# Fetching two weight matrices with 40 DMAs of four row blocks each, instead of 96 DMAs of one block

## The chip, the cores and the metric

The kernel runs on one core of a Trainium2 chip. The metric is the device time of one execution in microseconds; the kernel before took 446.88 us (median of 3 runs, 446.81 to 447.64). The profile is of one execution, whose span from the first to the last instruction is 445.8 us.

## The reference

An mLSTM cell (batch 4, 8 heads, 768 steps, head dimension 40) is followed by a multiplicative feed-forward block on 3072 tokens of 320 features.

```python
for t in range(S):                      # the cell, per batch and head
    m_new = np.maximum(f_gate + m, i_gate)
    C = exp(f_gate + m - m_new) * C + exp(i_gate - m_new) * outer(v, k)
    n = exp(f_gate + m - m_new) * n + exp(i_gate - m_new) * k
    y[t] = sigmoid(o_gate) * (C @ q) / max(abs(n @ q), 1)

x = y.transpose(0, 2, 1, 3).reshape(3072, 320)
a, b = x @ w1, x @ w2                   # w1, w2: 320 x 1024
out = (a * b @ w3) @ w_out              # w3: 1024 x 1024, w_out: 1024 x 320
```

The four weight matrices arrive as 64-bit floats, everything else as 32-bit floats. The kernel therefore sees each weight as two 32-bit words, and turns them into 32-bit floats itself.

## The kernel before

The program works in steps of one block of 128 tokens. In each step TensorE does the cell of that block and some matmuls of the feed-forward part, while the loads for later steps run. Since `(a * b @ w3) @ w_out` equals `a * b @ (w3 @ w_out)`, the kernel computes `w3o = w3 @ w_out` once, in the steps in which the weights come in.

A piece of a weight matrix goes through four stations: a raw buffer in SBUF that a DMA fills (`raw_tile`), a scaling of its two words on ScalarE (`scale`), the joining into a 32-bit float on VectorE (`to_f32`), and for w3 a turn of its 32 x 32 squares on VectorE. There are four raw buffers.

```python
def raw_tile(n, pieces):
    raw = idle.pop(0) if idle else wst.tile([128, n, 2], U32, name="raw", tag="raw", bufs=4)
    for r, src in pieces:                       # one DMA for each piece, on the SyncE queue
        dst = raw[r].rearrange("p n two -> p (n two)")
        if len(src.shape) == 3:
            dst = dst.rearrange("p (m n) -> p m n", m=2)
        nc.sync.dma_start(out=dst, in_=src)
    return raw

def scale(raw, early):
    lo, hi = raw[:, :, 0], raw[:, :, 1].bitcast(FP)
    nc.scalar.activation(out=hi, in_=hi, func=AF.Prelu, scale=2.0 ** -111, alpha=2.0 ** 32)
    # ... lo on ScalarE too (on VectorE for the first three)
```

The squares of w3 are turned within 32 partitions, so the order of w3's columns and w_out's rows over the partitions is chosen to suit that: partitions 32j to 32j+31 hold rows of w_out from its j-th quarter, and columns of w3 from their j-th quarter. Each such group of 32 partitions ("square") is filled by a DMA of its own.

```python
CQ = DFF // 4                                   # 256
squares = [slice(32 * j, 32 * (j + 1)) for j in range(4)]

elif kind == "wo":                              # i = 0..7; 128 rows of w_out
    dst, pieces = wo[:, i, :], [(square, wo_d[j * CQ + i * 32:j * CQ + (i + 1) * 32, :])
                                for j, square in enumerate(squares)]
else:                                           # w3: i = 0..7, part = 0, 1; 64 rows of w3
    dst, pieces = None, [(square, w3_d[i * 128 + part * 64:i * 128 + (part + 1) * 64, cols(j * CQ, CQ)]
                          .rearrange("(m r) n -> r m n", m=2)) for j, square in enumerate(squares)]
pend.append((dst, raw_tile(dst.shape[-1] if dst is not None else CW, pieces), i, part))
```

The SyncE queue issues these DMAs in program order between the other loads of a step. The main loop, cut to the loads and to what touches the raw buffers:

```python
for s in range(len(n_up)):
    if B <= s + 3 < NU: load_u(s + 3)           # pw: two DMAs
    if s + 2 < NU:
        load(s + 2)                             # k, q, v (q only while s + 2 < 10)
        load_o(s + 2)
    # ... cell and feed-forward matmuls of the step; fold() runs w3 @ w_out for finished blocks
    if N_DVE <= s + 1 < NU: gated = turn(s + 1) # turns k and q on VectorE
    # ...
    for _ in range(n_cvt[s] if s < len(n_cvt) else 0):
        convert()                               # scale if that is not done, then to_f32 (and turn w3)
    if s >= ahead:                              # ahead = 9
        while pend and len(scaled) < 2: scale_next()
    if N_DVE <= s + 2 < NU: load_turned(s + 2)  # eight DMAs
    while todo and fetched < converted + (2 if s < 2 else 3 if s < ahead - 1 else 4):
        fetch(*todo.pop(0)); fetched += 1
```

Of the kernel before, what the change touches and what calls it, by code (L numbers as in the profile page):

```python
# [16 lines left out]
def kernel(  # L17
# [37 lines left out]
    DM = H * D  # L55
# [101 lines left out]
    wo = const.tile([128, FO, DM], FP, name="wo")  # L157
# [5 lines left out]
    w1_d, w2_d, w3_d, wo_d = (x.bitcast(U32) for x in (moe_w1, moe_w2, moe_w3, moe_w_out))  # L163
# [3 lines left out]
    def raw_tile(n, pieces):  # L167
        raw = idle.pop(0) if idle else wst.tile([128, n, 2], U32, name="raw", tag="raw", bufs=4)
        for r, src in pieces:
            dst = raw[r].rearrange("p n two -> p (n two)")  # L170
            if len(src.shape) == 3:
                dst = dst.rearrange("p (m n) -> p m n", m=2)
            nc.sync.dma_start(out=dst, in_=src)  # L173
        return raw

# [15 lines left out]
    def cols(c0, n):  # L191
        return slice(2 * c0, 2 * (c0 + n))
# [1 line left out]
    every = slice(0, 128)  # L194

    CQ = DFF // 4
    squares = [slice(32 * j, 32 * (j + 1)) for j in range(4)]
    pend, scaled = [], []

    def fetch(kind, i, part):  # L200

        if kind == "w12":
            c0 = part * CW
            if i < 2 * KF:
                wt, src = ((w1, w1_d), (w2, w2_d))[i // KF]
                ko = i % KF
                dst, pieces = wt[:, ko, c0:c0 + CW], [(every, src[ko * 128:(ko + 1) * 128, cols(c0, CW)])]
            else:
                dst, pieces = wr[:, c0:c0 + CW], [(slice(j * REM, (j + 1) * REM), src[KF * P:DM, cols(c0, CW)])
                                                  for j, src in enumerate((w1_d, w2_d))]  # L210
        elif kind == "wo":
            dst, pieces = wo[:, i, :], [(square, wo_d[j * CQ + i * 32:j * CQ + (i + 1) * 32, :])
                                        for j, square in enumerate(squares)]
        else:
            dst, pieces = None, [(square, w3_d[i * 128 + part * 64:i * 128 + (part + 1) * 64, cols(j * CQ, CQ)]
                                  .rearrange("(m r) n -> r m n", m=2)) for j, square in enumerate(squares)]
        pend.append((dst, raw_tile(dst.shape[-1] if dst is not None else CW, pieces), i, part))


# [241 lines left out]
    w3o_words = w3o.rearrange("p f d -> p (f d)").bitcast(U32).rearrange("p (n two) -> p n two", two=2)  # L461
    load(0, slice(0, 2))
    fetch("w12", 0, 0)
    load(0, slice(2, 3))
    fetch("w12", 1, 0)
    load_o(0)
    fetch("w12", 2, 0)
    idle += [w3o_words[:, i * CW:(i + 1) * CW] for i in range(2)]
    fetch("w12", 3, 0)
# [360 lines left out]
```

## Time and profile before

| what | value |
|---|---|
| time | 446.88 us (446.81 to 447.64) |
| span of the profiled execution | 445.8 us |
| mean granted TensorE clock | 0.981 |
| moved by DMA | 52.72 MB, mean 118 GB/s |
| SyncE queue's packets under 512 bytes, of all 136555 | 109936 |
| VectorE busy, ScalarE busy | 306.3 us, 149.3 us |

The page gives busy times by engine, then rows of 40 equal slices of the span (11.1 us each), in which a digit is a busy share in tenths; then the DMA queues, the chain of work that ended last, the costliest groups of instructions, and the DMA issues with the KB of one and the median time from issue to landing. Queue q1 is SyncE's, q10 ScalarE's. PE is TensorE, DVE VectorE, ACT ScalarE, POOL GpSimd and SPq the queue of SyncE, where the issuing of a DMA is what takes time. L173 is the line of the `dma_start` in `raw_tile`, L180 the first scaling on ScalarE.

### The profile page before, as it was taken

The numbers are of one execution on the slowest core, as the hardware profiler recorded it, in microseconds if no ns is written. First come the engines' busy times: TensorE is split into PE (matmuls) and PEld (weight loads), VectorE is DVE, ScalarE is ACT, GpSimd is POOL, SyncE is SP. The second block draws the span as 40 slices with busy tenths as digits, with TensorE's granted clock in tenths as the row PEclk, the third lists the DMA queues.
The fourth block names the chain that finished last, engine by engine and source line by source line (L and its number), as shares of the span: only waits on it lengthen the run. The fifth ranks groups of instructions, "written<-read, shape, count | busy, mean of one in ns | idle before, by whom it ended". The sixth has DMA issues, their size and how long they took to land.

```text
span 445.8 us, 12871 instructions
## 1 busy us (share of the span) xinstructions
PE 423.7 (95%) x5271; PEld 335.5 (75%) x5271; DVE 306.3 (69%) x639; ACT 149.3 (34%) x407; POOL 81.7 (18%) x154
## 2 busy tenths in 40 slices
PE   4768989898999999999999999999999999999997
PEld 3656877787878878787877877778778777777774
DVE  5578387668866976696677949668699776444800
ACT  3766465445752454253212321213211111101110
POOL 3344043233211220222022203202020000000000
PEclk9995899999999999999999999999999999999999
DMA  8999989778988798697366466364111120000001
GB/s 203 182 175 201 200 142 170 172 176 166 205 198 186 147 180 177 161 165 140 83 116 148 102 132 140 76 136 109 50 35 35 39 46 16 15 16 15 1 30 44
DMA packets 136555, 52.72 MB, mean 118 GB/s; under 512 B 109936, under 2 KB 127536, under 8 KB 136496
## 3 DMA queue, kind: packets, MB, share of 16 engines
q1 hardware_dynamic: 132896, 47.87, 53.7%
q10 hardware_dynamic: 3600, 4.03, 2.7%
q8 instruction: 41, 0.67, 0.7%
q14 instruction: 18, 0.15, 0.1%
HBM read 46.07 MB, written 5.80 MB: 116 GB/s over the span
## 4 chain that ended last, share of the span: by engine, by line
PE 80%; DMA 5%; SPq 5%; ACT 3%; DVE 2%; POOL 2%; issue 2%; DVEq 0%; POOLq 0%
PE cell L92 22%; PE pa L92 18%; PE po L92 14%; PE pb L92 12%; PE wp L92 8%; PE p L92 5%; SPq L173 2%; SPq L128 2%; DMA raw<-in_moe_w_dram 2%; DMA o_in<-in_o_gate_dram 1%; DMA kbuf<-in_k_dram 1%; PE px L95 1%; POOL pw L279 1%; ACT pw L277 1%; ACT raw L180 1%
## 5 line engine op out<-in xcount | busy, mean ns | idle before, releaser
L92 PE MATMUL pa<-xT,w 128*128 128x256 f32 x240 | 62.1, 391 | 0.6 <-ACT xT L437 0.6
L92 PE MATMUL po<-w3o,ab 128*128 128x320 f32 x224 | 61.8, 433 | 0.0
L92 PEld LDWEIGHTS po<-w3o,ab 128*128 128x128 f32 x224 | 42.4, 190 | 17.3 <-issue 0.4
L306 POOL TENSOR_TENSOR state<-state,decay 128x164 f32<-128x164 f32 x40 | 19.7, 492 | 182.5 <-DVE den L387 168.2
L92 PEld LDWEIGHTS pa<-xT,w 128*128 128x128 f32 x240 | 45.7, 195 | 8.5 <-ACT xT L437 1.0
L92 PE MATMUL pb<-xT,w 128*128 128x256 f32 x192 | 45.9, 382 | 2.3 <-ACT kT L296 2.3
L583 DVE TENSOR_TENSOR ab<-pb,a_sb 128x512 f32<-128x512 f32 x24 | 16.6, 692 | 43.6 <-ACT a_sb L582 43.6
L279 POOL TENSOR_SCALAR_AFFINE_SELECT pw<-pw 64x512 f32<-64x512 f32 x48 | 34.4, 717 | 52.9 <-ACT pw L277 48.3
L92 PE MATMUL cell<-w3o,ab 128*128 128x320 f32 x160 | 44.0, 432 | 0.0
L92 PEld LDWEIGHTS pb<-xT,w 128*128 128x128 f32 x192 | 36.7, 192 | 8.2 <-ACT kT L296 3.1
L277 ACT ACTIVATE pw<-pw,aT 128x64 f32<-128x64 f32 x160 | 40.2, 336 | 2.8 <-ACT o_sb L685 2.8
L582 ACT ACTIVATE a_sb<-pa 128x512 f32<-128x512 f32 x24 | 14.3, 598 | 76.3 <-PE pb L92 76.3
L92 PEld LDWEIGHTS cell<-w3o,ab 128*128 128x128 f32 x160 | 30.4, 190 | 12.0
L630 DVE SCALAR_TENSOR_TENSOR a_sb<-pa,wo 128x512 f32<-128x512 f32 x12 | 8.3, 692 | 43.2 <-PE pa L92 43.2
L92 PE MATMUL pa<-xT,wr 64*64 64x256 f32 x384 | 36.8, 386 | 0.0
L92 PE MATMUL pb<-xT,wr 64*64 64x256 f32 x384 | 36.2, 379 | 0.0
L92 PE MATMUL wp<-wo,w3T 128*128 128x320 f32 x128 | 35.8, 432 | 0.0
L379 DVE TENSOR_TENSOR h<-cell,h 64x164 f32<-64x164 f32 x96 | 31.3, 326 | 1.8
L92 PEld LDWEIGHTS wp<-wo,w3T 128*128 128x128 f32 x128 | 23.7, 190 | 8.9
L92 PEld LDWEIGHTS pa<-xT,wr 64*64 64x64 f32 x384 | 19.0, 132 | 14.4 <-issue 8.4
L685 ACT COPY o_sb<-po 128x320 f32<-128x320 f32 x14 | 6.0, 427 | 67.4 <-PE po L92 67.4
L92 PEld LDWEIGHTS pb<-xT,wr 64*64 64x64 f32 x384 | 20.2, 133 | 3.0
(128 smaller groups left out, 722.8 us busy)
## 6 DMA issues: line engine op xcount, KB each, us to landing
raw<-in_moe_w_dram SPq DMA_DIRECT2D x64, 128.0 KB, 3.4
pw<-U_d SPq DMA_DIRECT2D x40, 128.0 KB, 3.7
kbuf<-in_k_dram SPq DMA_DIRECT2D x24, 160.0 KB, 4.5
vbuf<-in_v_dram SPq DMA_DIRECT2D x24, 160.0 KB, 5.1
o_in<-in_o_gate_dram SPq DMA_DIRECT2D x24, 160.0 KB, 4.8
out_dram<-o_sb ACTq DMA_DIRECT2D x24, 160.0 KB, 1.8
raw<-in_moe_w_dram SPq DMA_DIRECT2D x7, 512.0 KB, 5.6
raw<-in_moe_w_out_dram SPq DMA_DIRECT2D x32, 80.0 KB, 2.3
```

The lines of the kernel that those rows point to most:

```text
L92: in_order(nc.tensor.matmul(out, lhsT=lhsT, rhs=rhs, start=start, stop=stop))
L95: in_order(nc.tensor.transpose(out, in_, ident[0:n, 0:n]))
L128: nc.sync.dma_start(out=dst, in_=rows(src, n))
L173: nc.sync.dma_start(out=dst, in_=src)
L277: nc.scalar.activation(out=pw[:, h, :], in_=src[:, h, :], func=AF.Exp, bias=aT[:, c, b * H + h:b * H + h + 1])
L279: nc.gpsimd.affine_select(out=pw[r], in_=pw[r], compare_op=OP.is_ge, fill=0.0, base=0, pattern=[[0, H], [1, L]], channel_multiplier=-1)
L306: nc.gpsimd.tensor_tensor(out=new, in0=old, op=OP.mult, in1=decay[:, b * NP:(b + 1) * NP, 2 * c + x:2 * c + x + 1] .to_broadcast([P, NP, D1]))
L379: nc.vector.tensor_tensor(out=part, in0=ph[x][halves[e]], in1=part, op=OP.add)
L582: nc.scalar.mul(out=a_sb, in_=pa, mul=UP ** -2)
L583: nc.vector.tensor_tensor(out=ab_t[gr][j][:, fs[0]:fs[-1] + 1, t0:t0 + a_sb.shape[-1]], in0=pb, in1=a_sb, op=OP.mult)
L630: nc.vector.scalar_tensor_tensor(out=out, in0=p, scalar=UP ** -2, in1=q, op0=OP.mult, op1=OP.add)
L685: nc.scalar.copy(out=o_sb, in_=po)
```

## The change

The four DMAs of a w_out piece become one, and the four of a w3 piece become two. The source of each has three steps: the block j of four, the row of 32 within it, and the words of the row. The target is simply the 128 partitions with one run of words in each; the three-step source walks through it in the same order. For w3 the two halves m of a raw buffer (rows 0 to 31 and 32 to 63 of the piece) are each a DMA. It is meant to save the SyncE queue the issuing of 56 DMAs. The bytes, the runs of contiguous words and their places in SBUF are the same as before, and so is every instruction on the compute engines.

```diff
         for r, src in pieces:
-            dst = raw[r].rearrange("p n two -> p (n two)")
-            if len(src.shape) == 3:
-                dst = dst.rearrange("p (m n) -> p m n", m=2)
+            dst = (raw[:, r] if len(src.shape) == 3 else raw[r]).rearrange("p n two -> p (n two)")
             nc.sync.dma_start(out=dst, in_=src)
 ...
-    squares = [slice(32 * j, 32 * (j + 1)) for j in range(4)]
 ...
         elif kind == "wo":
-            dst, pieces = wo[:, i, :], [(square, wo_d[j * CQ + i * 32:j * CQ + (i + 1) * 32, :])
-                                        for j, square in enumerate(squares)]
+            dst, pieces = wo[:, i, :], [(slice(0, DM), wo_d.rearrange("(j c) n -> j c n", j=4)[:, i * 32:(i + 1) * 32, :])]
         else:
-            dst, pieces = None, [(square, w3_d[i * 128 + part * 64:i * 128 + (part + 1) * 64, cols(j * CQ, CQ)]
-                                  .rearrange("(m r) n -> r m n", m=2)) for j, square in enumerate(squares)]
+            dst, pieces = None, [(slice(m * CQ, (m + 1) * CQ), w3_d[r0:r0 + 32, :].rearrange("r (j n) -> j r n", j=4))
+                                 for m, r0 in enumerate(range(i * 128 + part * 64, i * 128 + (part + 1) * 64, 32))]
```

As built, the source of a w_out DMA is 4 x 32 x 640 words (steps 163840, 640, 1) and its target 128 x 1 x 640; the source of a w3 DMA is 4 x 32 x 512 words (steps 512, 2048, 1) and its target 128 x 1 x 512. Before, both sides were 32 x 640 for w_out and 32 x 2 x 512 for w3. The order of the instructions on the other queues does not change.

## The prediction

> **What bounds the kernel now.** I read the page first, for which engine fills the span and what the DMA queues carry. The trace then gave three further views: busy time by stretch, the timeline of the SyncE queue (which issues nearly every load), and the timeline of ScalarE, where the arriving weight pieces are first touched.
>
> ```profile
> span 445.8 us, 12871 instructions
> PE 423.7 (95%) x5271; PEld 335.5 (75%) x5271; DVE 306.3 (69%) x639; ACT 149.3 (34%) x407; POOL 81.7 (18%) x154
> ...
> DMA  8999989778988798697366466364111120000001
> ...
> q1 hardware_dynamic: 132896, 47.87, 53.7%
> q10 hardware_dynamic: 3600, 4.03, 2.7%
> ...
> PE 80%; DMA 5%; SPq 5%; ACT 3%; DVE 2%; POOL 2%; issue 2%; DVEq 0%; POOLq 0%
> ...
> raw<-in_moe_w_dram SPq DMA_DIRECT2D x64, 128.0 KB, 3.4
> ...
> out_dram<-o_sb ACTq DMA_DIRECT2D x24, 160.0 KB, 1.8
> ...
> raw<-in_moe_w_out_dram SPq DMA_DIRECT2D x32, 80.0 KB, 2.3
> ...
> gates<-in_i_gate_dram ACTq DMA_DIRECT2D x3, 32.0 KB, 2.0
> ```
>
> TensorE is busy for 95% of the span and makes 80% of the chain. The DMA row says that this isn't the whole story: for the first half of the span the 16 DMA engines are busy for seven to nine tenths of each slice, and in the last third hardly at all. So the kernel is bound by TensorE, with a first half in which the DMA engines are not far behind. The pieces that the change touches (64 issues for w3, 32 for w_out) all lie in that half.
>
> ```profile
> core 0: us, PE busy (x) PEld busy (x) DVE busy (x) ACT busy (x) POOL busy (x), PEclk, DMA share, GB/s
> ...
> 31.50:40.00 8.50, 7.27 (x167) 6.28 (x159) 6.40 (x17) 5.14 (x14) 1.83 (x3) 0.50 1.04 181
> ...
> 57.80:68.20 10.40, 9.06 (x177) 7.86 (x178) 8.94 (x19) 6.19 (x17) 4.65 (x8) 1.00 0.78 150
> ...
> 89.00:101.00 12.00, 12.00 (x206) 10.34 (x204) 7.97 (x19) 5.93 (x17) 3.66 (x6) 1.00 0.79 178
> ...
> 143.40:158.80 15.40, 15.40 (x225) 12.48 (x219) 11.58 (x24) 6.50 (x17) 3.31 (x6) 1.00 0.77 169
> ```
>
> The columns end with the granted clock, the DMA share and GB/s. From 112.5 us a step of the loop takes 15.4 us and TensorE fills all of it, with the DMA engines at about 0.8: the margin is a fifth.
>
> ```profile
> 57.82 5.53 SPq L173 DMA_DIRECT2D raw<-in_moe_w_out_dram x8
> ...
> 106.64 8.54 SPq L173 DMA_DIRECT2D raw<-in_moe_w_dram x16
> ...
> 183.73 3.60 SPq L173 DMA_DIRECT2D raw<-in_moe_w_dram x8
> ```
>
> ```profile
> 120.30 0.68 ACT L180 ACTIVATE raw<-raw 128x512 f32<-128x512 f32 x1 [1.46 <-DMA raw<-in_moe_w_dram]
> ...
> 194.18 0.67 ACT L184 ACTIVATE raw<-raw 128x512 uint32<-128x512 uint32 x1
> 194.75 0.45 ACT L437 COPY xT<-px 128x384 f32<-128x384 f32 x1
> ```
>
> The first w_out pieces are called for at 57.82 us, the last w3 pieces at 183.73. ScalarE scales each piece in program order, so a piece that comes late stops everything behind it on ScalarE, such as the copies that empty TensorE's banks. At 120.30 us it already waited 1.46 us for a w3 piece. There is little room for later landings.
>
> **What the Trainium skill says.** The page "DMA: Bandwidth & Descriptors", section "Why a DMA increments its semaphore by 16 and not by 1", has the decisive statement: a DMA is split over the largest number k of engines, at most 16, that divides the size of the slowest dimension (not of size 1) of both access patterns, and with a smaller k it uses the lowest-numbered engines. The trace of before fits k = 16 for every DMA. The ScalarE queue has 24 stores of 128 rows and 3 loads of 32 rows, 3168 rows; the page counts 3600 packets, and the 432 left are 27 issues times 16, one completion packet for each engine. The slowest dimensions there are 128 and 32. No DMA of the kernel before has a slowest dimension below 16, so nothing in it shows a smaller k. The section "Rules for kernel authors" of that page pulls both ways: it says to join many small transfers, which is what the change does, and to keep an outermost dimension that is a multiple of 16. The page "TensorE: Matmul & The Clock Gate", Part 1, says that the TensorE clock falls to half after an idle window of about 3.4 us; the stretch from 31.5 us above has 0.50, so long waits for data cost twice here.
>
> **The change part by part.**
>
> *Issues.* w_out goes from 32 issues to 8, w3 from 64 to 32: 56 fewer. The w3 issues take 3.60 us for eight in the timeline, 0.45 us each, so 25 us of the SyncE queue's time are saved. The chain has SPq at 5%, 22 us, of which the weight pieces' line L173 is 2%, 9 us. At most those 9 us could leave the path; more likely 3 to 5, as other waits end close by.
>
> *Engines per DMA.* The new source of a w_out piece is 4 x 32 x 640 words, that of half a w3 piece 4 x 32 x 512, with j = 4 outermost; the target has 128 partitions outermost. The largest number that divides 4 and 128 is 4. By that rule every new DMA runs on engines 0 to 3 alone. Bytes and rows stay: 1024 rows of 2560 bytes for w_out, 4096 of 2048 bytes for w3.
>
> *What a row costs one engine.* The trace has a record of each packet. The fastest tenth of the 2048-byte ones took 84 ns or less, of the 2560-byte ones 100 ns; the median of the 640-byte ones is 32 ns and the mean of the 160-byte ones 19 ns. A w_out piece has 128 rows: on 16 engines 8 rows each, 0.8 us; on 4 engines 32 rows, 3.2 us. A w3 piece (512 KB) has 256 rows: 16 rows each, 1.3 us, against 64 rows, 5.4 us.
>
> *What else these four engines carry.* Until the turned loads begin, a step loads k, q, v and o (4 x 1024 rows over 16 engines, 4 x 64 x 19 ns = 4.9 us) and the weights pw (2 x 64 rows, 8 x 84 ns = 0.7 us): 5.6. Later it is k, v, o (3.65), the turned k and q (1024 rows of 640 bytes, 64 x 32 ns = 2.05) and pw: 6.4 us. A later step with two w3 pieces therefore needs 10.8 + 6.4 = 17.2 us of engines 0 to 3, against 2.7 + 6.4 = 9.1 before and against TensorE's 15.4. Four engines become the bound while twelve stand idle.
>
> *The sum.* I treat engines 0 to 3 as one queue that is free at about 60.5 us (the o load issued at 56.87 has landed about then). Behind it come 8 w_out pieces, 26 us; 16 w3 pieces, 86 us; three early steps of other loads, 17 us; six later ones, 38 us. That makes 167 us, so the last w3 piece is through at about 228 us, and landed some 2 us after that. Before, its issue ended at 187.3 us and it landed in 3.4: 190.7. So it comes 39 us later. What can be absorbed: ScalarE's scaling starts 1.8 us after the landing, and the copy of px that follows (194.75) is needed by TensorE only when its banks come round, which I read as 4 to 5 us later. 39 less about 6 is 33 us. Freed issue time takes nothing off in a stretch that waits for four engines, and after the last piece the kernel is bound by TensorE as before. 446.9 + 33 = 480 us. Stalls at half clock may add a little: 481.
>
> It should not come evenly. The three single or double w_out steps add 2 to 4 us each; the worst is the sixteen-issue stretch at 106.64, where four w3 pieces come together: 21.6 us of engines 0 to 3 instead of 5.4. From there every step should be near 17 us instead of 15.4.
>
> **The rivals.**
> - *All 16 engines are kept.* Speaks for it: nothing in the trace shows a smaller k, and the transfer could be cut along the 128 target partitions. Then 25 us of SyncE time go, landings move little, and the time is 441 to 447 us. I give this about one in eight.
> - *Four engines, but hidden.* The loads run two steps ahead, four buffers hold w3, and once TensorE binds, DMA has a fifth to spare. If slack of 20 us is built up by 190 us, the loss is only 15 to 20: about 465. Against it: the 1.46 us wait at 120.30 and DMA shares near 0.8.
> - *Worse than the queue.* SyncE issues in order[...]; the early loads in the timeline took up to 4.81 us to issue one DMA (vbuf at 12.23). Loads of k, v and o would then wait behind w3 also where they are needed first, buffers come free late, and bubbles add to the 167 us. With TensorE at half clock: 495 to 515.
>
> **Range and chances.** Four engines give 465 to 510 by these; the working says 481. Sixteen engines give a result near 444. I leave that as the tail below the range: 457 to 510. Faster by over 2% needs 9 us, all that L173 has in the chain: 0.03. Within 2%: 0.12. Slower: 0.85.
>
> **What would show it.** Packets of the SyncE queue: 420 issues of 16 completion packets each lie in the 132896. With 4 of them for each of 40 new issues and 16 for the other 324 it is 131520; with 16 for all, 132000. The landing of a 256 KB w3 DMA: above 6 us for four engines, near 4 for sixteen. The DMA share between 60 and 220 us: lower than now although DMA binds, as twelve engines idle. The chain: DMA of raw and ScalarE's L180 in it, TensorE well below 80%. Steps near 17 us from 130 us on. I'm wrong if the packets come to 132000, or if they come to 131520 and the steps stay at 15.4 us.

## The result, and the profile after

The changed kernel took 496.52 us (median of 6 runs, 495.51 to 498.64) against 447.31 us before (446.81 to 448.03): a ratio of 1.110, with a 95% interval of 1.108 to 1.113. It is 49 us slower. The prediction said 481, in a range of 457 to 510.

The page of the changed kernel, cut to the rows that answer to those shown of before:

```profile
span 494.9 us, 12784 instructions
...
PE 433.6 (88%) x5271; PEld 340.3 (69%) x5271; DVE 305.2 (62%) x639; ACT 150.7 (30%) x407; POOL 81.7 (16%) x154
...
DMA  8999855545244544545567667365321111000001
...
q1 hardware_dynamic: 131520, 47.86, 43.9%
q10 hardware_dynamic: 3600, 4.03, 2.4%
...
PE 59%; DMA 15%; SPq 9%; DVE 5%; POOL 5%; issue 3%; ACT 3%; DVEq 0%; ACTq 0%; POOLq 0%
```

The SyncE queue has 131520 packets, to the packet the number for four completion packets on each of the 40 joined DMAs; 132000 would have meant sixteen. From the sixth slice to the 19th the DMA row has fallen to 4 or 5 tenths (once 2), where it had mostly 7 to 9, although the kernel now waits for DMA: the joined transfers leave most of the engines unused. TensorE's part of the chain fell from 80% to 59%, and DMA and SyncE rose to 24% together.

The busy time by stretch, three consecutive steps and the one before them (last columns: granted clock, DMA share, GB/s):

```profile
core 0: us, PE busy (x) PEld busy (x) DVE busy (x) ACT busy (x) POOL busy (x), PEclk, DMA share, GB/s
...
129.00:158.00 29.00, 17.38 (x219) 13.62 (x212) 11.60 (x23) 8.89 (x22) 3.31 (x6) 0.82 0.43 119
158.00:175.00 17.00, 15.64 (x215) 12.27 (x211) 11.59 (x23) 6.44 (x18) 3.31 (x6) 1.00 0.53 135
175.00:195.70 20.70, 17.23 (x219) 13.52 (x215) 11.59 (x23) 6.69 (x18) 3.31 (x6) 0.92 0.46 121
195.70:216.00 20.30, 17.43 (x219) 13.70 (x215) 11.60 (x23) 6.69 (x18) 3.31 (x6) 0.92 0.48 129
```

A step of 15.4 us has become one of 17 to 21, and the step that waits for four w3 pieces (129 to 158 us) takes 29. In the slow steps the clock is below 1, which is why TensorE is busy for 17 us with the same matmuls.

ScalarE's timeline shows what the steps wait for. The bracket is the idle time before an instruction and what ended it:

```profile
201.80 0.68 ACT L178 ACTIVATE raw<-raw 128x512 f32<-128x512 f32 x1 [2.57 <-DMA raw<-in_moe_w_dram]
...
207.64 0.68 ACT L178 ACTIVATE raw<-raw 128x512 f32<-128x512 f32 x1 [4.57 <-DMA raw<-in_moe_w_dram]
...
221.16 0.71 ACT L178 ACTIVATE raw<-raw 128x512 f32<-128x512 f32 x1 [1.69 <-DMA raw<-in_moe_w_dram]
...
226.64 0.67 ACT L178 ACTIVATE raw<-raw 128x512 f32<-128x512 f32 x1 [4.24 <-DMA raw<-in_moe_w_dram]
```

ScalarE now waits for both w3 pieces of these steps (L178 is the former L180). It takes up the two pieces of a pair 5.84 and 5.48 us apart, close to the 5.4 us of 64 rows on one engine. Such waits at this line add up to 47.8 us, where the kernel before had 2.4.

The timeline of the SyncE queue over one such step, from one call for w3 to the next:

```profile
153.93 2.60 SPq L171 DMA_DIRECT2D raw<-in_moe_w_dram  x4
156.64 1.81 SPq L148 DMA_DIRECT2D pw<-U_d  x2
158.50 0.58 SPq L128 DMA_DIRECT2D kbuf<-in_k_dram  x1
159.18 6.05 SPq L128 DMA_DIRECT2D vbuf<-in_v_dram  x1
165.27 3.53 SPq L142 DMA_DIRECT2D o_in<-in_o_gate_dram  x1
168.85 2.00 SPq L137 DMA_DIRECT2D gates<-in_k_dram  x4
170.90 1.85 SPq L137 DMA_DIRECT2D gates<-in_q_dram  x4
172.86 2.60 SPq L171 DMA_DIRECT2D raw<-in_moe_w_dram  x4
```

The queue has no gap of more than 0.11 us in these 18.9 us, though it issues four DMAs fewer than before. One issue for v takes 6.05 us and one for o 3.53. The same two in a step with w3 of the kernel before:

```profile
159.28 0.54 SPq L128 DMA_DIRECT2D vbuf<-in_v_dram  x1
159.86 1.49 SPq L142 DMA_DIRECT2D o_in<-in_o_gate_dram  x1
```

There v takes 0.53 or 0.54 us in all steps with two w3 pieces, and o 1.09 to 2.71. Against the shortest such issues, 0.53 and 0.37 us, some 8.7 us of the step are blocked. The semaphore records of the trace show what the blocked issues wait behind: in the five steps from here on, v's issue ends 0.2 to 0.5 us before the step's third w3 DMA has landed (165.23 and 165.45 us in this one), and o's 0.4 to 0.5 us after the fourth has (168.80 and 168.33). I read this as the lists in which the work of the four engines waits (their rings) being full; the trace does not name them.

### The profile page after: what moved, and what is told of

It is laid out like the page before. It is cut to its first block, busy times and chain, and to the rows that moved or that the text cites. A ratio compares the mean times of both kernels' runs of the same rounds, so it can differ in the third digit from the quotient of the medians.

```text
span 494.9 us, 12784 instructions
## 1 busy us (share of the span) xinstructions
PE 433.6 (88%) x5271; PEld 340.3 (69%) x5271; DVE 305.2 (62%) x639; ACT 150.7 (30%) x407; POOL 81.7 (16%) x154
## 3 DMA queue, kind: packets, MB, share of 16 engines
q1 hardware_dynamic: 131520, 47.86, 43.9%
## 4 chain that ended last, share of the span: by engine, by line
PE 59%; DMA 15%; SPq 9%; DVE 5%; POOL 5%; issue 3%; ACT 3%; DVEq 0%; ACTq 0%; POOLq 0%
PE cell L92 18%; PE pa L92 13%; PE po L92 12%; DMA raw<-in_moe_w_dram 10%; PE pb L92 8%; PE p L92 4%; POOL pw L275 3%; SPq L142 2%; DMA raw<-in_moe_w_out_dram 2%; SPq L137 2%; SPq L171 2%; PE wp L92 2%; SPq L128 2%; DMA o_in<-in_o_gate_dram 1%; DVE h L375 1%
## 5 line engine op out<-in xcount | busy, mean ns | idle before, releaser
L92 PE MATMUL pa<-xT,w 128*128 128x256 f32 x240 | 69.0, 424 | 25.7 <-ACT xT L433 24.1
L92 PEld LDWEIGHTS pa<-xT,w 128*128 128x128 f32 x240 | 49.7, 214 | 37.8 <-ACT xT L433 26.9
L92 PE MATMUL pb<-xT,w 128*128 128x256 f32 x192 | 49.0, 401 | 16.4 <-ACT kT L292 16.4
L92 PEld LDWEIGHTS pb<-xT,w 128*128 128x128 f32 x192 | 38.7, 203 | 23.5 <-ACT kT L292 17.6
L92 PEld LDWEIGHTS po<-w3o,ab 128*128 128x128 f32 x224 | 42.4, 190 | 17.3 <-issue 0.4
L178 ACT ACTIVATE raw<-raw 128x512 f32<-128x512 f32 (+1 forms) x32 | 20.2, 631 | 64.6 <-DMA raw<-in_moe_w_dram 47.8
```

What stands on the lines that cost most here:

```text
L92: in_order(nc.tensor.matmul(out, lhsT=lhsT, rhs=rhs, start=start, stop=stop))
```

## The experiments

Twelve runs of eleven kernels were made, in four batches, each batch beside runs of the kernel before on its own chip. Where totals differ by a few us only, I also compare the time between two marks of ScalarE's timeline, the copy of step 5 and the first one of step 16: the start-up before the first mark varies by some 4 us between runs, and the weights come in between the two. Before, that is 60.92 to 219.72, 158.8 us; after, 58.74 to 268.87, 210.1 us.

**Is it the number of engines? 40 DMAs of other shapes.** The joined DMAs keep their number, size, rows and three-step sources, but the outermost step counts 16, 8 or 4.

```diff
-wo_d.rearrange("(j c) n -> j c n", j=4)[:, i * 32:(i + 1) * 32, :]
+wo_d[i * 128:(i + 1) * 128, :].rearrange("(c j) n -> j c n", j=16)      # 8, 4
-w3_d[r0:r0 + 32, :].rearrange("r (j n) -> j r n", j=4)
+w3_d[i * 128:(i + 1) * 128, cols((2 * part + m) * CQ, CQ)].rearrange("(c j) n -> j c n", j=16)   # 8, 4
```

The weights then stand in another order in SBUF; nothing is left out.

> The changed kernel with the same 40 DMAs of the same sizes and rows, each with a source in three steps, but 16 x 8 rows instead of 4 x 32 (weights arrive in another order, so the output is not the reference's). If the DMA engines taken are the largest number that divides both outermost sizes, 16 are used: 443 to 448 us, 132000 packets on the SyncE queue. If a source in three steps, or joining pieces as such, is what costs, nothing improves: 490 to 500 us.

> The same with 8 x 16 rows. By the count of engines: 8 are used, 131680 packets on the SyncE queue; a w3 piece costs each of them 2.7 us, a later step 5.4 + 6.4 = 11.8 us, under TensorE's 15.4, so most is hidden: 447 to 456 us. If three steps as such cost: 490 to 500 us.

> Control for the kernels with 16 x 8 and 8 x 16 rows: the same choice of rows as theirs, but 4 x 32. If only the count of engines matters, it is like the changed kernel, 493 to 500 us, 131520 packets. If those were faster for their choice of rows: 450 to 465 us.

Measured: 452.6 us with 16 (ratio to before 1.009, interval 1.006 to 1.012), 464.1 with 8 (1.039, 1.033 to 1.045), 507.6 with 4 (1.130, 1.125 to 1.135). The page's line of the SyncE queue, for 16, 8 and 4 in this order:

```profile
q1 hardware_dynamic: 132000, 47.86, 54.2%
```

```profile
q1 hardware_dynamic: 131680, 47.86, 51.1%
```

```profile
q1 hardware_dynamic: 131520, 47.86, 43.9%
```

All three counts are those of the rule. The packet records of the traces show the engines at work too. Rows of 2560 bytes are w_out's alone. Between 60 and 250 us, whenever any of them is moving, four or five are moving at once for 29.0 of 35.0 us in the changed kernel, and hardly ever more than six; with 8 outermost it is eight or nine for 13.5 of 24.5 us; with 16 it goes up to 19. (The records of one engine overlap a little.) In the changed kernel's burst, from 126 to 139 us, several w3 DMAs wait together, and four or five rows move for 12.9 of the 13.0 us: the DMAs of this queue share the same four engines.

Three steps in a source cost nothing like 49 us; the engines do. Sixteen engines come out 5 us above what I expected. Eight engines lose 17 us, also more: in the profiled run, the slowest of four, the steps 9 to 11, which wait for the four w3 pieces called for together and for what queues behind them, take 17.0, 21.6 and 21.2 us, and from step 12 on they take 15.4. So the steady steps are hidden as worked out (11.8 us of work in 15.4), but the burst is not. The control with 4 is 11 us above the changed kernel, and above the range expected; it differs from it in the rows that an engine reads. That difference stays open.

**Is it joining, after all? Small DMAs on four engines.** The kernel before, with its 96 DMAs and nothing joined, but sources of 4 x 8 rows.

```diff
-wo_d[j * CQ + i * 32:j * CQ + (i + 1) * 32, :]
+wo_d[j * CQ + i * 32:j * CQ + (i + 1) * 32, :].rearrange("(c f) n -> f c n", f=4)
-w3_d[i * 128 + part * 64:i * 128 + (part + 1) * 64, cols(j * CQ, CQ)].rearrange("(m r) n -> r m n", m=2)
+w3_d[i * 128 + j * 32:i * 128 + (j + 1) * 32, cols(part * CW, CW)].rearrange("(c f) n -> f c n", f=4)
```

> The kernel before with its 96 small DMAs, nothing joined, but each with a source in three steps, 4 x 8 rows, so that 4 divides both outermost sizes and no larger number does (weights arrive in another order; w3's rows are 4096 bytes here, half as many). If the engines taken by a DMA are the whole cause, it is about as slow as the changed kernel: 485 to 500 us, with 129696 packets on the SyncE queue. If joining the pieces were the cause: 446 to 449 us.

Measured: 496.9 us (1.111, 1.105 to 1.117), as slow as the changed kernel, with

```profile
q1 hardware_dynamic: 129696, 47.86, 44.9%
```

as expected for four completion packets each. With the run of 16 outermost this settles the cause from both sides: joined on sixteen engines is within 1% of before, unjoined on four is all of the loss.

**Which matrix?** One part of the change at a time.

> Only w_out's pieces are joined, w3 as before. By the count of engines: 8 pieces of 3.2 instead of 0.8 us, 19 us more on engines 0 to 3 in the steps between 57 and 110 us, half of it hidden: 452 to 460 us, 132416 packets. If the whole loss comes from w3: 446 to 449 us.

> Only w3's pieces are joined, w_out as before. By the count of engines: 16 pieces of 5.4 instead of 1.3 us, 65 us more on engines 0 to 3, of which what TensorE's steps hide goes off: 478 to 490 us, 132000 packets. The two parts alone should add up to about the whole 49 us; if they share one wait they add up to more.

Measured: w_out alone 459.8 us (1.028, 1.026 to 1.031), 12.5 us above its own before of 447.3; w3 alone 489.7 us (1.095, 1.090 to 1.100), 42.4 above, both within the ranges expected and with the packets expected. Together 55 us, a little more than the 49 of both, which fits waits that the two share.

**Is TensorE's clock part of it?** TensorE is busy for 433.6 us instead of 423.7 with the same instructions. Extra matmuls, which nothing reads, were put where it stood still.

```diff
+if warm and (p is pb) == warm[0][1]:
+    for _ in range(warm.pop(0)[0]):
+        mm(cell[1][:, 0, 400:512], ident, ident[:, 0:112])
```

> The changed kernel with 352 extra matmuls of 112 columns, into a part of a bank that nothing reads, where TensorE stood still in steps 7, 9, 10, 12, 13 and 15. The changed kernel's TensorE is busy 9.9 us longer than before with the same instructions. If that is the half clock after each stall and lies on the path, the time falls by 6 to 10 us, to 486 to 491, with TensorE's granted clock back near 0.98. If the loads cover it: 496 to 499 us.

The first run was a miss: 524.9 us (1.172, 1.170 to 1.174). Its extra matmuls took 0.226 us each and outlasted the stalls; in step 7 the 58 took 13.1 us, for a stall of 6. It tells nothing about the clock. The second had 134 of them, sized by that duration.

> The run with extra matmuls again, with 134 of them instead of 352: one took 0.226 us and not the 0.095 us that it was sized by, so that the extra work outlasted the stalls it should fill. Now it is a little shorter than each stall of the changed kernel. If the half clock after a stall lies on the path: 486 to 491 us with a granted clock near 0.98. If not: 496 to 499 us.

Measured: 500.2 us (1.115, 1.111 to 1.119), no gain, though between 59 and 253 us the granted clock is 0.96, where the changed kernel has 0.90. Two of TensorE's waits in it:

```profile
153.26 1.99 PE L92 MATMUL pa<-xT,w 128*128 128x256 f32 x8 [1.32 <-ACT xT L433]
172.77 3.58 PE L92 MATMUL pa<-xT,w 128*128 128x256 f32 x8 [3.82 <-ACT xT L433]
```

Step 10 (153.26) starts at full clock after a wait of 1.32 us, where the changed kernel had waited 11.62 us and then ran its eight matmuls in 3.71. From the mark in step 5 to that of step 10 it took 95.4 us instead of 99.0. But the next step waits 3.82 us for the loads, in which the changed kernel waited 0.78, and from mark to mark both take 210 us. What the clock gives, the loads take back. My reading that the slow clock costs time of its own fell.

**Does the order of issues matter?** In the changed kernel, w3 is called for before the eight turned loads of the same step, instead of after them.

```diff
+        while todo and fetched < ...: fetch(*todo.pop(0)); fetched += 1
         if N_DVE <= s + 2 < NU:
             load_turned(s + 2)
-        while todo and fetched < ...: fetch(*todo.pop(0)); fetched += 1
```

> The changed kernel with a step's w3 pieces called for before its eight turned loads. SyncE takes 3.85 us to issue the turned loads, which keep an engine busy for 2.05, so engines 0 to 3 may run dry before w3 is called for. If they do, steps come down by up to 1.8 us and the time to 486 to 491 us. If engines 0 to 3 never run dry: 495 to 498 us.

Measured: 489.7 us (1.093, 1.089 to 1.097), 7 us below the changed kernel. From mark to mark it takes 200.0 us, 10 less. But the last ten w3 pieces still come at 18.8 us a pair, against 19.2 in the changed kernel (by ScalarE's starts on them), so most of the gain comes once, up to the burst of four pieces, and not as 1.8 us in each step: the time falls into the range expected, but not in the way expected. The timeline and the waits of its SyncE queue show why:

```profile
168.51 2.91 SPq L171 DMA_DIRECT2D raw<-in_moe_w_dram  x4
171.46 4.50 SPq L137 DMA_DIRECT2D gates<-in_k_dram  x4
176.00 7.56 SPq L137 DMA_DIRECT2D gates<-in_q_dram  x4
183.67 1.14 SPq L148 DMA_DIRECT2D pw<-U_d  x2
```

```profile
SPq L137 <- DMA raw<-in_moe_w_dram: 36.0, 18, 3.2
```

Now the turned loads are the blocked ones, 12.06 us for eight issues that take 3.85 in the changed kernel, and here the trace names the w3 transfers as what ended 36 us of those waits (between 100 and 240 us). They are waits for a semaphore: in the trace SyncE's DMAs use eight semaphores in turn, and an issue waits until the DMA of eight issues before has landed. Those at 176.91, 180.46 and 183.25 us start 0.02 us after a w3 DMA's last increment. So this is another wait than that of v and o above. VectorE waits for the turned loads in turn (3.6 to 6.5 us a step), and frees the raw buffers later. The blocking moves; it does not go.

**Another queue.** The joined DMAs are called for by GpSimd, so that their issues are no longer in SyncE's order.

```diff
-nc.sync.dma_start(out=dst, in_=src)
+(nc.gpsimd if len(src.shape) == 3 else nc.sync).dma_start(out=dst, in_=src)
```

> The changed kernel with its 40 joined DMAs called for by GpSimd instead of SyncE; all else the same. In the changed kernel SyncE stands for about 8.6 us of each 18.9 us step at issues that take 3.5 to 6 us, which I read as full rings of engines 0 to 3. If that blocking makes the steps longer than the 17.2 us of the four engines' own work, and GpSimd's DMAs use the same four, steps come near 17 us: 478 to 488 us. If GpSimd's DMAs are laid over all engines: 446 to 455 us. If neither holds, or GpSimd's own work is held up: 495 us or more.

Measured: 469.4 us (1.049, 1.046 to 1.052), between the two expectations. From step 12 on the steps take 15.4 us but for one of 16.8. ScalarE still waits for w3, 16.8 us in all, and a 256 KB w3 DMA lands after 9.8 us (median). Its queues:

```profile
q1 hardware_dynamic: 126240, 36.85, 44.4%
q0 software_dynamic: 10880, 11.07, 11.9%
```

10880 packets are 272 for each of the 40 DMAs: by their sizes, 64 of data (two rows each), 16 completion packets and 192 of 8 bytes. The records of the data packets show another spread over the engines. Between 60 and 240 us, whenever any of w3's 4096-byte packets is moving, more than five are moving at once for 54.6 of 78.2 us, up to 17, and most often 4, 8 or 12. I read the counts in fours as DMAs that take four engines each, but not the same four, where SyncE's all share four. Over half of the loss goes with the change of queue. That the spread is wider is shown; how much of the gain is due to it, and how much to SyncE's shorter issues, this run does not separate: v's issue now takes 0.5 to 0.8 us, but the eight turned loads still take 11.38 us at 141.67 us.

**What is an issue worth?** The change was to save SyncE's time. The kernel before with each of its 96 DMAs cut in two of 16 partitions, and the 40 DMAs on sixteen engines once more, in 14 runs.

```diff
-for j, square in enumerate(squares)
+for j in range(4) for h in (0, 16)            # partitions 32j+h to 32j+h+15, on sixteen engines as before
```

> The kernel before with each of its 96 DMAs cut into two of 16 partitions, still on 16 engines: 96 more issues of 0.45 us, 43 us more of the SyncE queue's time. If issuing these pieces is on the path, as the change supposes: 465 to 490 us. If the queue has that much room: 447 to 450 us. Packets of the SyncE queue: 134432.

> The 40 DMAs on 16 engines once more, to see whether saving 56 issues gains anything where no engine is lost: the first run had 452.6 us, 0.9% above before. If joining itself has a cost: again 450 to 453 us. If that was the chip or chance: 444 to 448 us.

Measured: 483.0 us with 192 DMAs (1.077, 1.073 to 1.082), and its SyncE queue has

```profile
q1 hardware_dynamic: 134432, 47.87, 50.2%
...
169.78 8.72 SPq L173 DMA_DIRECT2D raw<-in_moe_w_dram  x16
```

16 issues of 0.545 us for one step's two w3 pieces: 96 more issues cost 35 us. But 56 fewer gain nothing: 450.7 us (1.0057, 1.0036 to 1.0077). In that run the waits of the SyncE queue at the line of the pieces, between 55 and 200 us, begin with

```profile
SPq L171 <- DVE wo L186: 14.2, 4, 6.6
SPq L171 <- DVE w L187: 6.1, 6, 1.9
```

and come to 25 us, against 10 in the kernel before. They wait for VectorE to free a raw buffer. SyncE gets to the pieces sooner and stands there for the buffer. Why it is 2 to 3 us slower rather than equal stays open; from mark to mark it takes 161.7 us, 2.9 more than before. The kernel also has the other choice of rows, which on four engines cost 11 us. So what 56 fewer issues would be worth with the rows of before is not shown.

## Why the prediction was right in kind and a third too small

- **Four engines per joined DMA.** Right, and shown from both sides: the packet counts of the changed kernel, of the kernels with 16 and 8 outermost and of the small DMAs on four are exact, the rows move four, eight or sixteen at a time, and the times follow. That they are the lowest-numbered four is what the page "DMA: Bandwidth & Descriptors" of the Trainium skill states in the section "Why a DMA increments its semaphore by 16 and not by 1"; no run here shows which four.
- **The cost of a row.** Right: in the burst the first five w3 DMAs land 2.67 to 2.68 us apart, two to a piece, 5.4 us as predicted. ScalarE's starts on two successive pieces are 5.5 to 6.6 us apart where it waits for the second, as other loads' rows go in between.
- **The sum: "I treat engines 0 to 3 as one queue".** This is the term that was too small. The working had the last w3 piece landed at about 230 us; it landed at 245.4, 15 us later. Row costs give nothing of that. The four engines are not one queue that is always full: in each of five steps, after the fourth w3 DMA has landed, no w3 row moves for 5.8 to 7.1 us, while the packets of the other loads take only 3.6 to 3.9 us of an engine (mean of the 16). SyncE, blocked until that landing, must then issue the turned loads, and w3 is called for only after those. A pair of pieces therefore comes every 19.2 us and not every 17.2, some 10 us in five pairs. How the other 5 us divide, in the steps with w_out and the burst, no run separates. I had this as a rival ("Worse than the queue"), whose range, 495 to 515 us, holds the measured time, and gave it nothing in the sum. Calling for w3 earlier in a step is worth 7 us, and a pair still takes 18.8 us.
- **What can be absorbed.** Too large by a few us: ScalarE starts on the last piece 53.0 us later than before (245.49 against 192.49), and 51.3 of them are lost from mark to mark. The working had about 6 absorbed.
- **"Stalls at half clock may add a little".** They appear, with TensorE busy 9.9 us longer, but in the run with 134 extra matmuls, which has more than half of the lost clock back, the time stays where it is.
- **The saved issues.** The working gave 0 where four engines bind, and the rival with sixteen engines 441 to 447 us. Sixteen engines gave 450.7, with other rows: the saved time becomes waiting for raw buffers. No run here bears out the rival's gain.
- **Where the loss sits.** Right in place: by the marks of ScalarE's timeline, steps 6 to 8, with w_out, lose 9.9 us, steps 9 and 10, with the burst, 9.2 and 13.6, and the five that follow 1.8 to 5.2 each, where the prediction had near 2. From step 16 on a step takes 15.4 us again.

## What to carry to other kernels

Before joining DMAs, write down the outermost size of both sides of the access pattern: what divides both decides how many engines carry the transfer (4, 8 and 16 here), and a source with 4 outermost gives up three quarters of them, at 80 KB as at 320. On SyncE's queue such DMAs also share the same four, so several at once do not help. The completion packets in the profile tell it at once (packets less rows, by DMA). And an issuing queue that is full without gaps is not yet the bound: see first whether the time freed would meet a full buffer.

## What the runs showed of the hardware that was not expected

- A DMA that fills a few engines also holds up the queue that issued it: single issues of 160 KB loads took 3.5 to 6 us behind four-engine transfers, while the mean share of the 16 engines was near 0.5. The kernel before has such issues where the share is near 1 (v at 35.84 us, 3.06 us; share 1.04).
- The same 40 DMAs with 4 outermost take 469 us in all when GpSimd calls for them and 497 when SyncE does. GpSimd's have up to 17 data packets moving at once, SyncE's mostly four or five.
- Four engines with other rows (every fourth row instead of a block of columns of each row) cost 11 us more. The two pieces of a pair are as far apart as in the changed kernel (5.4 to 6.6 us against 5.5 to 6.6), but a pair comes every 20.9 us instead of 19.2.
